# Transformer block on one core: prologue with w_mod's first part on one queue, one rstd for four tiles, two tiles' statistics on ScalarE, K before Q, and no early stop for PV without V

## The chip, the cores and the metric

The kernel runs on one core of a Trainium2 chip. The metric is the device time in microseconds (us), as the median of several runs. The engines are named as in the profile: PE (TensorE, matmuls; PEld is its weight load), ACT (ScalarE), DVE (VectorE), POOL (GpSimd), SP (SyncE, which here only issues transfers).

## The reference

One transformer block with adaptive layer norm, on 2048 tokens of 512 values, 32 heads of 16 and a feed-forward width of 1792, all in bfloat16:

```
mod = silu(c) @ w_mod                      # six rows of 512: sa, ca, ga, sb, cb, gb
h   = layernorm(x) * (1 + ca) + sa
q, k, v = split(h @ wqkv)                  # 32 heads of 16
x   = x + ga * (softmax(q k^T / 4) v @ wo)
h   = layernorm(x) * (1 + cb) + sb
x   = x + gb * ((gelu(h @ w_gate) * (h @ w_up)) @ w_down)
```

## The kernel before, in words

A recorder takes every instruction in the order of the program, keeps for every tile who wrote and read it, and adds the semaphore waits that follow. Two engines that read the same PSUM bank are ordered as well: the later reader waits for the earlier. Each engine executes its instructions in the order in which they were recorded.

The program has three stretches.

The *prologue* (`prologue`, L558 on) loads c, x and the first columns of the weights, computes silu(c), the first eight modulation columns (`mod_cols`, 32 matmuls that read w_mod's first 1024 columns), the layer norm statistics of the first four token tiles, their normalized copies, their transposes and modulation (into `hT`), and K and Q of the first 128 columns for the first 512 tokens. Statistics of a tile are two DVE instructions (`ln_stat`); `ln_rstd` is two small POOL instructions for a range of tiles; `ln_norm` is one DVE instruction per tile. `warm_up(n)` gives PE n dummy products, of four matmuls each. Transfers are issued on two queues, SP's and ACT's; a transfer issued on ACT occupies ACT's instruction stream while it is issued. The first scores need K (`km[0]`, the tile kme, in which every second head is masked) and Q (`qT`).

The *stream* (`stream`, L1185 on) is written by a planner at build time. The scores are worked through in items: one item is one head's scores for 128 keys and 512 queries, one PSUM bank. A round is four items, the four heads of one unit for one key tile. PE writes scores into three banks, then into two (later three) others; ACT turns each set into E with one exp. At positions from 30 on, some rounds (quads) are taken off ACT: DVE computes their four banks into uint16 and makes the shifted copies, partly with POOL. PV products (E times V, into `ps_pv` or a score bank) follow when their four items are there. In the first 128 items the planner goes through four groups of four key tiles for the first two units, so K of a new group of tokens must be there every 32 items.

Between scores the planner puts side work on PE: V, transposes, K and Q of later tokens and columns, then the modulation rows, and later the output projection and the feed-forward part of finished query sets. Side work is paced by a credit that grows with each item taken (the side work still to do, divided by the items up to its due position). It is forced when something needs it (`require`). Small steps on DVE, POOL, ACT and SP hang in a list of tasks and are taken when the planner's model has the engine free. `side_first` (L752) is the first piece of side work: V of the first tokens, then the statistics and norms of the other twelve tiles as tasks, then for each group its transposes, K and V.

`pv_next` lists the PV rounds that could run. If V of the round is not computed, it has this rule, where `tq` is the time at which the next score banks are free and `pos` the number of items taken:

```python
if ("v", r * (512 // u[3]) // 4, u[1] // 2) not in self.have:
    if tq is not None and pos < SOON:
        break
    x = 0.0
```

A candidate with `x = 0.0` counts as ready; if it is taken, `pv` forces the side work up to V. It is taken when PE's last instruction used the array in column strips (as V's products do) and the credit is at most 1536, or when no score banks can be free soon.

The *tail* (`tail`) finishes the last two query tiles.

Of the kernel before, what the change touches and what calls it, by code (L numbers as in the profile page):

```python
# [5 lines left out]
ACT = mybir.ActivationFunctionType  # L6
ALU = mybir.AluOpType
# [6 lines left out]
P = 128  # L14
S_TOK = 2048
D = 512
# [53 lines left out]
URGENT = 6  # L70
LAG = 40
SOLO = 2
SOON = 12
CLOSE = 48
BACK = 8
END = (0, None)
# [397 lines left out]
class _Kernel(_Recorder):  # L474
# [12 lines left out]
    def alloc(self):  # L487
# [49 lines left out]
        self.st6 = sb("st6", [P, 2, 6], FP32)  # L537
        self.rstd = sb("rstd", [P, NT], FP32)
        self.half = sb("half", [P, 4], FP32)
        self.crow = dreg[:, 9 * D:10 * D]  # L540
        self.tcol = sb("tcol", [P, NDC], FP32)
        self.sc_bf = sb("sc_bf", [P, NDC], BF16)
        self.scbc = sb("scbc", [P, NDC, P], BF16)[:, :, :]
        self.modA = sb("modA", [P, 8], FP32)
# [13 lines left out]
    def prologue(self):  # L558
        sp, act, pe, dve, pool = "sp", "act", "pe", "dve", "pool"
        xv = self.A_x.rearrange("b (t p) d -> p (b t) d", p=P)  # L560
        wmv = self.w_mod.rearrange("(a p) n -> p a n", p=P)
        wqv = self.A_wqkv.rearrange("(a p) (k n) -> p a k n", p=P, k=3)
        wq4 = self.wqkv.rearrange("p a (k n) -> p a k n", k=3)
        self.dma(sp, self.crow[0:1, :], self.c, "c")
        self.dma(act, self.xs[:, 0:2, :], xv[:, 0:2, :], "x0")
        self.dma(sp, self.xs[:, 2:4, :], xv[:, 2:4, :], "x1")
        self.dma(act, self.wmod[0][:, 0:2, :], wmv[:, 0:2, 0:1024], "wm0")
        self.dma(sp, self.wmod[0][:, 2:4, :], wmv[:, 2:4, 0:1024], "wm2")
        for k, q in ((1, sp), (0, act), (2, sp)):
            self.dma(q, wq4[:, :, k, 0:P], wqv[:, :, k, 0:P], "wq%d" % k)  # L570
        self.dma(act, self.xs[:, 4:8, :], xv[:, 4:8, :], "x2")
        self.dma(sp, self.xs[:, 8:12, :], xv[:, 8:12, :], "x3")
        self.dma(sp, self.xs[:, 12:16, :], xv[:, 12:16, :], "x4")
        for k in range(3):
            self.dma(sp, wq4[:, :, k, P:D], wqv[:, :, k, P:D], "wr%d" % k)
        self.dma(sp, self.wmod[1], wmv[:, :, 1024:3072], "wm1")

        self.memset(dve, self.warm, 0.0)
        self.memset(dve, self.ones, 1.0)
        self.memset(dve, self.half[:, :], -0.5)  # L580
        self.memset(dve, self.pv[:, :], 0.0)
        self.memset(dve, self.scp[:, SC - 1, :], 0.0)
        self.warm_up(7)
        self.memset(pool, self.ident[:, :], 0.0)
        self.affine_select(self.ident[:, :], [[-1, P]], ALU.not_equal, 1.0, 0, 1)
        self.memset(pool, self.rm4, 1.0)
        self.affine_select(self.rm4, [[-32, 4]], ALU.is_ge, 0.0, -16, 1)
        self.affine_select(self.rm4, [[32, 4]], ALU.is_ge, 0.0, 31, -1)
        self.reduce(self.rm[:, 1:2], self.rm4, mybir.AxisListType.X, ALU.add)
        self.ts(dve, self.rm[:, 0:1], self.rm[:, 1:2], -1.0, 1.0, ALU.mult, ALU.add)  # L590
        self.memset(pool, self.vaug[:, :, :].rearrange("p t (h c) -> p t h c", c=VW)[:, :, :, DH:VW], 1.0)

        for dc in range(NDC):
            self.mm(self.scp[:, 0, dc:dc + 1], self.crow[0:1, P * dc:P * dc + P], self.ones[0:1, 0:1])
        self.warm_up(14)
        self.act(self.tcol[:, :], self.scp[:, 0, 0:NDC], ACT.Tanh, scale=0.5)
        for t in range(2):
            self.ln_stat(t)
        self.ln_rstd(0, 2)
        self.stt(self.tcol[:, :], self.tcol[:, :], 1.0, self.scp[:, 0, 0:NDC], ALU.add, ALU.mult)  # L600
        self.ts(dve, self.sc_bf[:, :], self.tcol[:, :], 0.5, None, ALU.mult)
        for t in range(2, 4):
            self.ln_stat(t)
        self.ln_rstd(2, 4)
        self.mod_cols(self.scp[:, 1, 0:8], 0)
        for t in range(4):
            self.ln_norm(t, self.tb1[:, 0, t, :])
        self.copy(dve, self.modA[:, :], self.scp[:, 1, 0:8])
        self.ts(dve, self.modA[:, 4:8], self.modA[:, 4:8], 1.0, None, ALU.add)
        self.warm_up(3)  # L610
        kb, qb = self.pv[:, :], self.scp[:, 1, :]
        for dc in range(NDC):
            pt = self.scp[:, 2 + dc, :].bitcast(BF16)[:, 0:512]
            for t in range(4):
                self.transpose(pt[:, P * t:P * t + P], self.tb1[:, 0, t, P * dc:P * dc + P], self.ident[:, :])
            self.modulate(dve if dc % 2 == 0 else act, self.hT[:, dc, 0:512], pt, self.modA, dc)
        for dci in range(NDC):
            self.proj_part(kb, 512, 0, dci)
            self.proj_part(qb, 0, 0, dci)
        self.ts(dve, self.km[0][:, 0, 0:512], kb, self.rm[:, 0:1], None, ALU.mult)  # L620
        self.act(self.qT[:, 0, 0:512], qb, ACT.Copy, scale=Q_SCALE)
        self.ts(dve, self.km[1][:, 0, 0:512], kb, self.rm[:, 1:2], None, ALU.mult)

    def warm_up(self, n):
        for _ in range(n):
# [38 lines left out]
                        self.sc_bf[:, dc:dc + 1], start=(dc == 0), stop=(dc == NDC - 1))  # L664
        self.whole = False

    def proj_part(self, bank, col, g, dci):
        self.mm(bank, self.wqkv[:, dci, col:col + P], self.hT[:, dci, 512 * g:512 * g + 512],
                start=(dci == 0), stop=(dci == NDC - 1))

    def done(self, key):
        if not self.dry:
# [79 lines left out]
    def side_first(self):  # L752
        def stats(tiles):
            for t in tiles:
                self.task([lambda t=t: self.ln_stat(t)], ("st", t))

        def norms(t0):
            g = t0 // 4
            self.task([("pool", lambda: self.ln_rstd(t0, t0 + 4))]
                      + [lambda t=t: self.ln_norm(t0 + t, self.tb1[:, g % 2, t, :]) for t in range(4)], ("ln", g),  # L760
                      self.after([("st", t) for t in range(t0, t0 + 4)]))
        yield from self.side_v(0, 0)
        if not self.dry:
            stats([4, 5, 6, 7])
            norms(4)
        if not self.dry:
            stats([8, 9, 10, 11])
            norms(8)
            stats([12, 13, 14, 15])
        for g in range(1, 4):  # L770
            yield from self.until(("ln", g))
            for h in range(2):
                yield from self.side_t(lambda t: self.tb1[:, g % 2, t, :], 4, h,
                                       lambda dc: self.hT[:, dc, 512 * g:512 * g + 512], self.modA)
            if g == 1 and not self.dry:
                norms(12)
            yield from self.side_k(g, 0)
            yield from self.side_v(g, 0)
# [406 lines left out]
    def stream(self):  # L1185
# [76 lines left out]
        def pv_next():  # L1262

            res = []
            for k in open_rounds():
# [5 lines left out]
                    break  # L1271
                src = [self.slot[g0 + j] for j in range(4)]
                if ("v", r * (512 // u[3]) // 4, u[1] // 2) not in self.have:
                    if tq is not None and pos < SOON:
                        break
                    x = 0.0
                else:
                    x = self.probe(lambda: pv(rnd, 0, src))
# [457 lines left out]
```

## Time and profile before

| | |
|---|---|
| median of 3 runs | 807.23 us (806.83 to 807.97) |
| the profiled execution | 806.83 us, span 805.0 us |
| PE, DVE, ACT, POOL busy | 749.6, 671.0, 773.7, 277.7 us |
| first exp starts | 13.51 us |
| exps of two banks | 407, 1122 ns each |
| exps of three banks | 271, 1542 ns each |
| granted PE clock, mean | 0.999 |

A line of a group of instructions reads: source line, engine, operation, output tile and input tile with their shapes, count, then busy time in us and mean ns of one, then the idle time of the engine just before them and what ended most of it. A timeline line reads: start in us, length in us, engine, line, operation, tiles, count, and in brackets the idle time before it and its releaser; neighbouring instructions of one kind are merged. The line of GB/s divides the time asked for into 40 equal slices. A line of transfers ends with the size of one and the time from issue to landing. Line numbers are mostly those of helpers (L368 a matmul, L381 an ACT instruction, L393 a DVE or POOL tensor-scalar, L421 and L425 the statistics, L635 and L637 `ln_rstd`), so tiles tell the instructions apart: `ps_sc` holds scores and prologue products, `ps_mi` side work and warm-ups, `mreg` w_mod at first, `wreg` wqkv, `hreg` hT, `xs` x, `dreg` the normalized copies.

### The profile page before, as it was taken

The page shows a single profiled execution, that of the slowest core. Times are in us where ns is not written, and L with a number is a line of the kernel's source. Part 1 is how long each engine was busy: PE and PEld are TensorE (multiplying, and loading weights), DVE is VectorE, ACT ScalarE, POOL GpSimd, SP SyncE. Part 2 cuts the span into 40 slices and gives each one's busy share as a digit, 9 for nine tenths or more (in the row PEclk, how much of TensorE's full clock was granted, in tenths as well). Part 3 has the DMA queues.
Part 4 walks back from the last instruction along what each step waited for, and adds up shares of the span by engine and source line. Part 5 has one row for each costly group of instructions (what it writes and reads, how often), then busy time and mean ns, then how long its engine had stood idle before and what let it go on. Part 6 is the DMA issues. An engine that isn't in the chain of part 4 may idle for free.

```text
span 805.0 us, 27412 instructions
## 1 busy us (share of the span) xinstructions
PE 749.6 (93%) x12250; PEld 267.6 (33%) x12254; DVE 671.0 (83%) x1216; ACT 773.7 (96%) x728; POOL 277.7 (34%) x172
## 2 busy tenths in 40 slices
PE   8899999998899999999999899999999899999987
PEld 3333333322222222222222222222344342454455
DVE  7878898978898989988688998989778986677873
ACT  5999999999999999999999999999999999999982
POOL 3110335365546172456556346134262010000310
PEclk9999999999999999999999999999999999999999
DMA  9101000000022121111003111110123221120100
GB/s 310 58 9 19 10 10 16 10 16 10 16 55 68 35 55 36 48 41 29 24 27 108 36 52 51 48 42 17 42 59 89 63 75 37 34 75 14 23 9 14
DMA packets 58632, 36.03 MB, mean 45 GB/s; under 512 B 17977, under 2 KB 55090, under 8 KB 58514
## 3 DMA queue, kind: packets, MB, share of 16 engines
q1 hardware_dynamic: 56914, 32.84, 15.0%
q8 instruction: 96, 1.57, 0.8%
q10 hardware_dynamic: 1600, 1.44, 0.6%
q14 instruction: 22, 0.18, 0.1%
HBM read 29.62 MB, written 2.61 MB: 40 GB/s over the span
## 4 chain that ended last, share of the span: by engine, by line
ACT 89%; PE 8%; DVE 3%; issue 0%; DVEq 0%
ACT E L381 85%; PE ps_sc L368 4%; ACT wreg L381 3%; PE ps_mi L368 3%; PE ps_pv L368 1%; DVE mreg L393 1%; DVE kmo L402 0%; DVE xs L385 0%; DVE wreg L385 0%; PE ps_sc L372 0%; DVE hreg L393 0%; ACT L381 0%; DVE vaug L402 0%; DVE dreg L393 0%; DVE kme L393 0%
## 5 line engine op out<-in xcount | busy, mean ns | idle before, releaser
L381 ACT ACTIVATE E<-ps_sc 128x1024 bf16<-128x1024 f32 (+2 forms) x686 | 748.2, 1282 | 15.6 <-PE ps_sc L368 15.0
L393 POOL TENSOR_SCALAR mreg<-dreg 128x2048 uint16<-128x2048 uint16 x93 | 175.3, 1902 | 260.7 <-DVE mreg L393 105.7
L393 DVE TENSOR_SCALAR dreg<-ps_sc 128x512 uint16<-128x512 f32 x253 | 171.6, 685 | 34.3 <-PE ps_sc L368 31.8
L368 PE MATMUL ps_sc<-qT,kme 32*128 32x512 bf16 (+2 forms) x1313 | 168.3, 332 | 18.3 <-ACT E L381 15.1
L368 PE MATMUL ps_sc<-qT,kmo 32*128 32x512 bf16 (+2 forms) x1313 | 173.7, 332 | 9.7 <-ACT E L381 8.5
L368 PE MATMUL ps_pv<-E,vaug 128*17 128x512 bf16 (+2 forms) x2112 | 150.4, 327 | 0.8 <-DVE osb L402 0.5
L393 POOL TENSOR_SCALAR mreg<-mreg 128x2048 uint16<-128x2048 uint16 x46 | 86.7, 1902 | 138.8 <-DVE mreg L393 47.1
L368 PE MATMUL ps_pv<-mreg,vaug 128*17 128x512 bf16 (+2 forms) x1704 | 121.6, 337 | 1.7 <-DVE mreg L393 1.0
L393 DVE TENSOR_SCALAR mreg<-ps_sc 128x512 uint16<-128x512 f32 x126 | 85.4, 686 | 18.9 <-PE ps_sc L368 17.5
L368 PE MATMUL ps_mi<-wreg,mreg 128*32 128x512 bf16 (+1 forms) x1280 | 92.4, 372 | 4.4 <-DVE wreg L398 1.3
L368 PEld LDWEIGHTS ps_sc<-qT,kme 32*128 32x128 bf16 x1313 | 45.0, 91 | 143.7 <-ACT E L381 115.4
L368 PEld LDWEIGHTS ps_sc<-qT,kmo 32*128 32x128 bf16 x1313 | 45.7, 91 | 127.8 <-ACT E L381 109.3
L393 DVE TENSOR_SCALAR mreg<-dreg 128x2048 uint16<-128x2048 uint16 x117 | 76.8, 682 | 1.7 <-PE ps_pv L368 1.4
L368 PEld LDWEIGHTS ps_pv<-E,vaug 128*17 128x17 bf16 x2112 | 43.9, 89 | 61.5 <-issue 48.8
L368 PEld LDWEIGHTS ps_pv<-mreg,vaug 128*17 128x17 bf16 x1704 | 38.1, 89 | 36.8 <-issue 13.2
L402 DVE CAST wreg<-ps_mi 128x512 bf16<-128x512 f32 x49 | 33.5, 684 | 10.5 <-PE ps_mi L368 10.3
L368 PEld LDWEIGHTS ps_mi<-wreg,mreg 128*32 128x32 bf16 x1280 | 26.7, 95 | 44.0 <-issue 18.8
L368 PE MATMUL ps_mi<-hreg,wreg 128*32 128x512 bf16 x480 | 39.5, 385 | 0.0
L393 DVE TENSOR_SCALAR mreg<-mreg 128x2048 uint16<-128x2048 uint16 x59 | 38.4, 682 | 1.1 <-PE ps_pv L368 1.0
L398 DVE SCALAR_TENSOR_TENSOR wreg<-wreg,ps_mi 128x512 bf16<-128x512 bf16 x49 | 33.4, 682 | 6.5 <-PE ps_mi L368 5.1
L635 POOL TENSOR_SCALAR mv<-mv 128x4 f32<-128x4 f32 (+2 forms) x11 | 2.6, 239 | 94.5 <-DVE mv L425 93.9
L385 DVE TENSOR_TENSOR wreg<-wreg 128x1024 bf16<-128x1024 bf16 (+1 forms) x56 | 34.1, 616 | 0.5
(149 smaller groups left out, 670.8 us busy)
## 6 DMA issues: line engine op xcount, KB each, us to landing
mreg<-in_B_w_up_dram SPq DMA_DIRECT2D x22, 256.0 KB, 2.9
mreg<-in_B_w_gate_dram SPq DMA_DIRECT2D x15, 256.0 KB, 3.0
rb<-scr_rec SPq DMA_DIRECT2D x96, 32.0 KB, 1.8
dreg<-in_B_w_down_dram SPq DMA_DIRECT2D x9, 256.0 KB, 3.0
mreg<-in_w_mod_dram SPq DMA_DIRECT2D x1, 2048.0 KB, 13.3
mreg<-in_B_w_down_dram SPq DMA_DIRECT2D x8, 256.0 KB, 2.7
out_dram<-xs SPq DMA_DIRECT2D x16, 128.0 KB, 1.7
osb<-osb SPq DMA_DIRECT2D x48, 32.0 KB, 2.0
```

The costliest lines, as they stand in the source:

```text
L368: return self.rec("pe", lambda e: e.matmul(out, lhsT, rhs, start=start, stop=stop, tile_position=tp), [lhsT, rhs], [out], cost=(n, int(rhs ...
L381: return self.rec("act", lambda e: e.activation(out, in_, func, scale=scale, **kw), rd, wr, cost=self.cost("act", out, [in_], "act"))
L385: return self.rec(eng, lambda e: e.tensor_tensor(out, a, b, op), [a, b], [out], cost=self.cost(eng, out, [a, b], "tt"))
L393: return self.rec(eng, lambda e: e.tensor_scalar(out, a, s1, s2, **kw), rd, [out], cost=self.cost(eng, out, [a], "ts"))
L398: return self.rec("dve", lambda e: e.scalar_tensor_tensor(out, a, s, b, op0=op0, op1=op1), rd, [out], cost=self.cost("dve", out, [a, b], " ...
L402: return self.rec(eng, lambda e: e.tensor_copy(out, in_), [in_], [out], cost=self.cost(eng, out, [in_], "ts"))
L635: self.rec("pool", lambda e: e.tensor_scalar(v, v, EPS, None, op0=ALU.add), [v], [v], cost=200)
```

## The change

- w_mod's first 1024 columns were loaded as two halves, one on each queue; now as one transfer on SP. The second x transfer of ACT's queue follows x0 directly; of the three first wqkv parts the K part goes to SP and the Q and V parts to ACT; the last x transfer moves from SP to ACT.
- The statistics of tiles 4 and 5 are computed in the prologue on ACT, as two passes each with a sum (`act_stat`), and turned into mean and variance by three small DVE instructions (`act_stat_fin`). Those of tiles 6 and 7 are computed in the prologue on DVE, after the modulation.
- One `ln_rstd` for tiles 0 to 3 in place of two for two tiles.
- Warm-ups: 16 in place of 14 before the modulation columns, 2 behind them and none in place of 3 before the transposes.
- K and Q of the first 512 tokens: K's products all first, into a score bank; then ACT makes kmo and DVE kme from it; then Q's products. Before, the products alternated, DVE made kme and kmo, and K's bank was ps_pv.
- `side_first`: the norms of tiles 4 to 7 are put in the list before V, and need no statistics any more.
- The rule with SOON is gone from `pv_next`.

```diff
-        self.dma(act, self.wmod[0][:, 0:2, :], wmv[:, 0:2, 0:1024], "wm0")
-        self.dma(sp, self.wmod[0][:, 2:4, :], wmv[:, 2:4, 0:1024], "wm2")
-        for k, q in ((1, sp), (0, act), (2, sp)):
-            self.dma(q, wq4[:, :, k, 0:P], wqv[:, :, k, 0:P], "wq%d" % k)
+        self.dma(sp, self.wmod[0], wmv[:, :, 0:1024], "wm0")
         self.dma(act, self.xs[:, 4:8, :], xv[:, 4:8, :], "x2")
+        for k in range(3):
+            self.dma(sp if k == 1 else act, wq4[:, :, k, 0:P], wqv[:, :, k, 0:P], "wq%d" % k)
         self.dma(sp, self.xs[:, 8:12, :], xv[:, 8:12, :], "x3")
-        self.dma(sp, self.xs[:, 12:16, :], xv[:, 12:16, :], "x4")
+        self.dma(act, self.xs[:, 12:16, :], xv[:, 12:16, :], "x4")
...
-        self.warm_up(14)
+        self.warm_up(16)
         self.act(self.tcol[:, :], self.scp[:, 0, 0:NDC], ACT.Tanh, scale=0.5)
+        for t in range(4, 6):
+            self.act_stat(t)
         for t in range(2):
             self.ln_stat(t)
-        self.ln_rstd(0, 2)
         self.stt(self.tcol[:, :], self.tcol[:, :], 1.0, self.scp[:, 0, 0:NDC], ALU.add, ALU.mult)
         self.ts(dve, self.sc_bf[:, :], self.tcol[:, :], 0.5, None, ALU.mult)
         for t in range(2, 4):
             self.ln_stat(t)
-        self.ln_rstd(2, 4)
+        self.ln_rstd(0, 4)
         self.mod_cols(self.scp[:, 1, 0:8], 0)
+        self.warm_up(2)
...
-        self.warm_up(3)
-        kb, qb = self.pv[:, :], self.scp[:, 1, :]
...
-        for dci in range(NDC):
-            self.proj_part(kb, 512, 0, dci)
-            self.proj_part(qb, 0, 0, dci)
-        self.ts(dve, self.km[0][:, 0, 0:512], kb, self.rm[:, 0:1], None, ALU.mult)
-        self.act(self.qT[:, 0, 0:512], qb, ACT.Copy, scale=Q_SCALE)
-        self.ts(dve, self.km[1][:, 0, 0:512], kb, self.rm[:, 1:2], None, ALU.mult)
+        for t in range(6, 8):
+            self.ln_stat(t)
+        self.proj_k(0, 0, self.scp[:, 2, :], "both")
+        self.proj_q(0, 0, self.scp[:, 3, :], act)
+        self.act_stat_fin(4, 6)
+
+    def act_stat(self, t):
+        self.act(self.E[:, 0, :], self.xs[:, t, :], ACT.Copy, accum=self.asum[:, 0, t - 4:t - 3])
+        self.act(self.E[:, 0, :], self.xs[:, t, :], ACT.Square, accum=self.asum[:, 1, t - 4:t - 3])
+
+    def act_stat_fin(self, a, b):
+        m, q, t = self.asum[:, 0, a - 4:b - 4], self.asum[:, 1, a - 4:b - 4], self.nwt[:, a:b]
+        self.ts("dve", self.mv[:, a:b, 0], m, 1.0 / D, None, ALU.mult)
+        self.stt(t, m, 1.0 / D, self.mv[:, a:b, 0], ALU.mult, ALU.mult)
+        self.stt(self.mv[:, a:b, 1], q, 1.0 / D, t, ALU.mult, ALU.subtract)
...
+    def proj_k(self, g, dc, bank, how):
+        self.proj(bank, 512 + P * dc, g)
+        sl = slice(512 * g, 512 * g + 512)
+        if how == "both":
+            self.act(self.km[1][:, dc, sl], bank, ACT.Copy, scale=self.rm[:, 1:2])
...
+        self.ts("dve", self.km[0][:, dc, sl], bank, self.rm[:, 0:1], None, ALU.mult)
...
-                      self.after([("st", t) for t in range(t0, t0 + 4)]))
+                      self.after([("st", t) for t in range(max(8, t0), t0 + 4)]))
+        if not self.dry:
+            norms(4)
         yield from self.side_v(0, 0)
-        if not self.dry:
-            stats([4, 5, 6, 7])
-            norms(4)
...
-                    if tq is not None and pos < SOON:
-                        break
```

## The prediction

> **What bounds the kernel now.** I read the busy shares first, then the chain that ended last, then the groups of instructions by shape.
>
> ```profile
> PE 749.6 (93%) x12250; PEld 267.6 (33%) x12254; DVE 671.0 (83%) x1216; ACT 773.7 (96%) x728; POOL 277.7 (34%) x172
> ...
> ACT 89%; PE 8%; DVE 3%; issue 0%; DVEq 0%
> ```
>
> ```profile
> L381 ACT ACTIVATE E<-ps_sc 128x1024 bf16<-128x1024 f32 x407 | 399.9, 1122 | 0.5 <-PE ps_sc L368 0.5
> L381 ACT ACTIVATE E<-ps_sc 128x1536 bf16<-128x1536 f32 x271 | 391.6, 1542 | 2.6 <-PE ps_sc L368 2.1
> L381 ACT ACTIVATE wreg<-wreg 128x1024 bf16<-128x1024 bf16 x21 | 24.0, 1158 | 0.0
> ```
>
> ACT carries the chain: once the first exp has started, the 686 exps follow each other with hardly an idle microsecond. So the time is the start of the first exp, plus the sum of the exps, plus the few gaps between them, plus a tail after 780 us that the diff does not touch. Next I read the timeline of ACT alone, from 12 us on, for the start and the gaps.
>
> ```profile
> 12.33 0.60 ACT L381 ACTIVATE qT<-ps_sc 128x512 bf16<-128x512 f32 x1 [0.91 <-PE ps_sc L368]
> 13.51 13.66 ACT L381 ACTIVATE E<-ps_sc 128x1536 bf16<-128x1536 f32 x12 [0.58 <-PE ps_sc L368]
> 28.70 31.57 ACT L381 ACTIVATE E<-ps_sc 128x1536 bf16<-128x1536 f32 x31 [1.53 <-PE ps_sc L368]
> ```
>
> The first exp starts at 13.51. There is one gap of 1.53 us, at 27.17, where the first four key tiles are used up; the timeline of all engines shows K of the second four arriving late:
>
> ```profile
> 27.14 0.69 DVE L402 CAST kmo<-ps_mi 128x512 bf16<-128x512 f32 x1 [0.38 <-PE ps_mi L368]
> 27.87 0.35 DVE L393 TENSOR_SCALAR kme<-kmo,rm 128x512 bf16<-128x512 bf16 x1
> 28.26 0.35 DVE L393 TENSOR_SCALAR kmo<-kmo,rm 128x512 bf16<-128x512 bf16 x1
> 28.28 0.39 PE L368 MATMUL ps_sc<-qT,kme 32*128 32x512 bf16 x1 [0.87 <-DVE kme L393]
> ```
>
> The change moves both numbers, and a third place between them. The prologue in the timeline (DVE, POOL, PE) and the transfers of the first 30 us give the prices:
>
> ```profile
> 7.66 0.95 PE L368 MATMUL ps_sc<-sc_bf,mreg 128*128 128x1 bf16 x32
> 8.54 0.83 PE L368 MATMUL ps_mi<-dreg 128*32 128x512 bf16 x12
> ```
>
> ```profile
> 18.70 0.24 POOL L635 TENSOR_SCALAR mv<-mv 128x4 f32<-128x4 f32 x1 [10.10 <-DVE mv L425]
> 19.02 1.03 POOL L637 TENSOR_TENSOR rstd<-mv,half 128x4 f32<-128x4 f32 x1
> ```
>
> ```profile
> GB/s 0 0 34 243 343 406 412 380 355 292 281 306 308 301 359 347 350 338 328 328 326 370 370 414 399 399 404 421 365 367 217 46 37 0 22 0 0 0 0 0
> ...
> mreg<-in_w_mod_dram ACTq DMA_DIRECT2D x1, 512.0 KB, 4.6
> mreg<-in_w_mod_dram SPq DMA_DIRECT2D x1, 512.0 KB, 5.8
> ```
>
> **The change, part by part.** *w_mod's first part on one queue.* Now its halves, issued at 1.24 and 1.67, land at 5.84 and 7.47, and the modulation columns start on PE at 7.66, 0.19 later. After, the whole 1.05 MB stands on SP behind c and x1, while ACT's queue carries x0, x2 and two wq parts. Adding up the 0.75 us slices above, the core had moved 1.85 MB by 7.5 us, 2.06 by 8.25, 2.29 by 9.0, 2.52 by 9.75, 2.75 by 10.5. It lands at the earliest when x0, x1, x2 and itself are in (2.10 MB: 8.4 us), at the latest when both queues have moved the 1.31 MB that SP's needs (2.62 MB: 10.1 us). I take the middle, 9.3: neither end is nearer to a row.
>
> [...]
>
> *One rstd for four tiles instead of two for two.* The last of the four aggregates ends at 7.40 in both. Four columns took 0.24 + 1.03 on POOL, with the norms starting 1.50 after the aggregate; four norms took 1.35 there (20.11 to 21.46). So 7.40 + 1.50 + 1.35 = 10.25 for the last norm, against 9.38 now.
>
> *The meeting of both on PE.* Columns from 9.5 to 10.4; two warm-ups behind them 0.5 (three took 0.76) to 10.9; the first quarter of the transposes 0.27, and 0.1 to the first modulate: 11.3, now 9.76. The norms (10.25) are then hidden; if the transfer lands by 8.7 they set 10.6 instead.
>
> *ACT's statistics for tiles 4 and 5.* Four passes of 0.60 to 0.70 (512 columns from PSUM, 598 ns; from SBUF, 695 ns), 2.8 at most, in an ACT gap of 5.16 before its first modulate. x2 should land between 5.84 and 7.5, where the w_mod halves landed, so they end by 10.3, before ACT's modulate at 11.5: nothing, unless x2 lands after 8.7; then microsecond for microsecond. ACT also issues five transfers instead of four. Four took 0.43 to 0.53 each; a fifth 0.5 to 1.36 (the rows of SP's later ones), so the table load and tanh come 0.1 to 0.9 later and DVE, which reaches tanh's reader at 5.42, waits 0.4 at most: hidden, as the norms have 0.6 to spare. SP loses two issues and x4; its later weight loads move up, nobody waits for them.
>
> [...]
>
> *K first, then Q; one more pass.* Now K and Q alternate and the last Q group starts at 11.89. After, from 11.3: ACT's two modulates (1.45, begun 0.21 behind DVE's) end at 12.96; K's last group starts at 13.06, and four Q groups of 0.215 follow, the last at 13.92, ending at 14.31. qT takes 0.60 on ACT: 14.36 to 14.96, now 12.33 to 12.93. Beside it ACT does K's odd copy first (13.5 to 14.1); the even copy on DVE must wait for that, since the recorder orders readers of a bank on different engines. It runs 14.2 to 14.95; behind it the two statistics of tiles 6 and 7 (2 x 0.87, from 12.3 to 14.05) are hidden, by 0.1 only. wq1 follows w_mod on SP; one such part took 1.6, which gives 11.1 to 11.8, beside the 11.9 at which K starts. First QK 0.14 after qT, exp 0.44 later: 15.55, **+2.05**, bounds +1.4 (w_mod hidden) and +2.85 (10.1).
>
> *SOON removed.* After two rounds of QK (5 items) the first PV round has its four slots, but V does not exist. Now the planner breaks off there. After, V's first part puts PE in column mode with credit 273 x 3 + 284 x 2 - 512 = 876, under 1536, so PV is placed at once, V is forced, and PV stands in PE's order ahead of the third QK. Its fourth matmul needs the second exp. QK then starts only when that exp has ended: 0.05 for the release (14.96 to 15.01), 0.32 between starts when the mode changes (19.53 to 19.85), 0.44 to the exp: **+0.8**. Ends: 0 (QK placed first) and 1.5 (PV also waits for V's cast, 0.69 more).
>
> *Statistics of 4 to 7 gone from the stream, norms put ahead of V.* POOL can start at 15.4 instead of 18.70, relative to the first exp 5 us earlier. The gap of 1.53 needs 1.5, so K is no longer late. What is late next at such a boundary? At the next one, 71.52, the gap is 0.38; I let that remain: **-1.15** (ends -1.53 and 0).
>
> *DVE freed.* 4 x 0.87 = 3.4 us of DVE work leave the stream. The planner may give DVE one quad more (four items off ACT, 4 x 1.34/3 = 1.8 us), or, replanned from other times, one less. I take 0, ends -1.8 and +1.8.
>
> Sum: 2.05 + 0.8 - 1.15 = +1.7. The profiled execution took 806.83 (805.0 of span, 1.8 around it), so 808.5; the median of the runs is 0.40 above it, so **808.9**.
>
> **The rivals.** *Freed DVE takes quads (ends on the other side).* Place: 28 to 37 us, where DVE's first bank of a quad (31.38) is six microseconds from the second (37.37), with statistics, norms and modulates between. For it: three of those statistics would be gone. Against: from 30 to 50 us DVE is busy 15.7 of 20, so free time alone does not make quads. Price 1.8 each: one gives 807.1, two 805.3, faster; it decides from the second.
>
> *The gap at 27 us stays*, because side work is paced by credit and forced only when needed: +1.15, 810.0; with the late transfer too, 810.9. Against: K's chain gains far more than the gap.
>
> *The prologue's delay is smaller*: w_mod hidden and the PV order harmless, so 1.4 + 0 - 1.15: about 807.5, no difference.
>
> *The two starts add up with a lost quad*: 808.9 + 1.8 = 810.7.
>
> **How the numbers follow.** Two runs of this kernel can be told apart from about 0.2%, 1.6 us. My sum has 0.45 (807.9 to 809.7: two thirds of it beyond 808.84); gap stays or quad lost 0.27, slower; smaller delay 0.10, same; quads taken 0.18, of which 0.12 faster. Faster 0.12, same 0.32, slower 0.56. The range leaves out a tenth on each side: the end with nearly two quads taken and the top of the lost-quad case, 806.4 to 811.2.
>
> **What would show it.** First exp near 15.5, modulation columns on PE near 9.5 (right if between 8.7 and 10.3); a gap of 0.8 before the third exp with PV ahead of QK in PE's order; no gap over 0.5 near 29 to 31; the count of DVE's uint16 reads of score banks within four of now. I am wrong if the exps change in number, or if w_mod lands before 8.4.

## The result and the profile after

The changed kernel takes 812.75 us (811.46 to 812.88, 4 runs) against 807.39 (806.83 to 807.97, 4 runs): a ratio of 1.0063, with a 95% interval of 1.0045 to 1.0080. It is 5.4 us slower. The forecast had the sign and the places, but 1.7 us; the time lies above the top of its range, 811.2.

The page of the changed kernel, busy times and the chain that ended last:

```profile
PE 749.8 (92%) x12266; PEld 268.0 (33%) x12270; DVE 673.1 (83%) x1224; ACT 779.3 (96%) x734; POOL 246.4 (30%) x153
...
ACT 90%; PE 7%; DVE 2%; DMA 1%; issue 0%; SPq 0%; DVEq 0%
```

ACT is the chain as before, and it is busy 5.6 us longer. The exps by shape (count, then busy us and mean ns):

```profile
L380 ACT ACTIVATE E<-ps_sc 128x1536 bf16<-128x1536 f32 x280 | 406.6, 1546 | 2.5 <-PE ps_sc L367 1.8 <-PE ps_mi L367 0.3
L380 ACT ACTIVATE E<-ps_sc 128x1024 bf16<-128x1024 f32 x396 | 393.3, 1126 | 0.9 <-PE ps_sc L367 0.8
```

280 x 3 + 396 x 2 = 1632 score banks go through ACT. Before, 271 x 3 + 407 x 2 and a single one made 1628. The four more are one quad that DVE no longer gets: its uint16 reads of score banks went from 420 (253 + 126 + 27 + 14, by tile) to 416 (244 + 124 + 32 + 16). The timeline of ACT:

```profile
7.89 0.63 ACT L380 ACTIVATE E<-xs 128x512 bf16<-128x512 bf16 x1 [2.79 <-DMA xs<-in_A_x_dram]
...
10.69 0.19 ACT L380 ACTIVATION_READ_ACCUMULATOR E<-xs 128x1 f32 x1
12.12 1.48 ACT L380 ACTIVATE hreg<-ps_sc,modA 128x512 bf16<-128x512 bf16 x2 [1.24 <-PE ps_sc L371]
14.66 0.69 ACT L380 ACTIVATE kmo<-ps_sc,rm 128x512 bf16<-128x512 f32 x1 [1.06 <-PE ps_sc L367]
16.05 0.60 ACT L380 ACTIVATE qT<-ps_sc 128x512 bf16<-128x512 f32 x1 [0.70 <-PE ps_sc L367]
17.23 2.37 ACT L380 ACTIVATE E<-ps_sc 128x1536 bf16<-128x1536 f32 x2 [0.58 <-PE ps_sc L367]
20.61 53.05 ACT L380 ACTIVATE E<-ps_sc 128x1536 bf16<-128x1536 f32 x51 [1.02 <-PE ps_sc L367]
```

The first exp starts at 17.23 in place of 13.51. There is a new gap of 1.02 before the third exp, and the 1.53 at 27 us is gone. PE's timeline shows why the start is late:

```profile
7.71 0.82 PE L367 MATMUL ps_mi<-dreg 128*32 128x512 bf16 x12
10.04 0.94 PE L367 MATMUL ps_sc<-sc_bf,mreg 128*128 128x1 bf16 x32 [1.51 <-DMA mreg<-in_w_mod_dram]
10.91 0.61 PE L367 MATMUL ps_mi<-dreg 128*32 128x512 bf16 x8
11.46 1.32 PE L371 MATMUL ps_sc<-ident,dreg 128*128 128x128 bf16 x16
12.70 3.29 PE L367 MATMUL ps_sc<-hreg,wreg 128*32 128x512 bf16 x32
```

PE sits idle for 1.51 us until w_mod has landed, and later the 16 transposes take 1.32 and the 32 products of K and Q 3.29. Before, the transposes took 1.07, and the same 32 products ran from 10.36 to 12.28:

```profile
9.31 1.07 PE L372 MATMUL ps_sc<-ident,dreg 128*128 128x128 bf16 x16
10.36 0.40 PE L368 MATMUL ps_pv<-hreg,wreg 128*32 128x512 bf16 x4
...
11.89 0.39 PE L368 MATMUL ps_sc<-hreg,wreg 128*32 128x512 bf16 x4
```

Stretches of one microsecond (length, busy time and count of PE, PEld, DVE, ACT and POOL, then the granted PE clock, the share of the DMA engines and GB/s) show the clock of that time:

```profile
11.00:12.00 1.00, 1.00 (x18) 0.57 (x18) 0.44 (x3) 0.00 (x0) 0.00 (x0) 1.00 1.10 347
12.00:13.00 1.00, 1.00 (x14) 0.67 (x15) 1.00 (x3) 0.89 (x2) 0.00 (x0) 0.56 1.10 344
13.00:14.00 1.00, 1.00 (x16) 0.36 (x16) 0.96 (x3) 0.59 (x1) 0.00 (x0) 0.50 1.10 331
14.00:15.00 1.00, 1.00 (x16) 0.43 (x12) 0.51 (x2) 0.34 (x1) 0.00 (x0) 0.50 1.12 334
15.00:16.00 1.00, 1.00 (x20) 0.36 (x12) 0.55 (x1) 0.34 (x1) 0.00 (x0) 0.73 1.08 333
```

The clock granted to PE is halved from 12.1 to 15.5 us. In the trace of before it is 1.00 in every such stretch from 4 to 40 us.

One table holds all profiled executions. The medians of before that the ratios refer to lie between 807.2 and 807.5. *First* is the start of the first exp. *Exps* is ACT's time from there to the table load at the end of the stream, less *gaps* (its idle stretches in the stream, as the timeline lists them). *Tail* is the rest of the span. Each row adds up to its span, as the tail is what is left.

| kernel | median us | ratio to before (95%) | first | exps | gaps | tail | span | banks on ACT |
|---|---|---|---|---|---|---|---|---|
| before | 807.39 | | 13.51 | 762.40 | 2.08 | 26.97 | 805.0 | 1628 |
| changed | 812.75 | 1.0063 (1.0045 to 1.0080) | 17.23 | 764.29 | 2.42 | 26.97 | 810.9 | 1632 |
| e1 warm-ups | 812.67 | 1.0059 (1.0040 to 1.0077) | 16.15 | 764.22 | 4.62 | 26.97 | 812.0 | 1632 |
| e2 queues alone | 809.76 | 1.0026 (1.0016 to 1.0036) | 15.19 | 762.43 | 2.08 | 26.96 | 806.7 | 1628 |
| e3 7 warm-ups | 810.31 | 1.0035 (1.0020 to 1.0050) | 13.43 | 762.74 | 4.25 | 26.96 | 807.4 | 1628 |
| e4 SOON back | 812.16 | 1.0047 (1.0031 to 1.0063) | 16.69 | 765.01 | 2.80 | 26.98 | 811.5 | 1632 |
| e5 changed again | 813.13 | 1.0071 (1.0057 to 1.0085) | 16.68 | 764.30 | 2.97 | 26.97 | 810.9 | 1632 |
| e6 101 quads | 813.86 | 1.0083 (1.0070 to 1.0097) | 13.50 | 769.07 | 2.08 | 26.97 | 811.6 | 1644 |
| e7 statistics back | 812.17 | 1.0058 (1.0045 to 1.0072) | 16.40 | 761.87 | 3.31 | 28.98 | 810.6 | 1624 |
| e8 no SOON | 808.67 | 1.0018 (1.0008 to 1.0027) | 14.72 | 760.82 | 1.64 | 28.98 | 806.2 | 1624 |
| e9 1 warm-up | 809.37 | 1.0032 (1.0018 to 1.0046) | 14.94 | 762.71 | 3.97 | 26.97 | 808.6 | 1628 |
| e10 changed, other plan | 808.31 | 1.0009 (1.0000 to 1.0018) | 15.72 | 756.85 | 4.66 | 29.75 | 807.0 | 1612 |
| e11 BACK = 9 | 802.99 | 0.9948 (0.9933 to 0.9963) | 13.58 | 755.64 | 2.72 | 28.97 | 800.9 | 1612 |
| e12 no SOON, other plan | 806.32 | 0.9988 (0.9975 to 1.0000) | 13.89 | 754.67 | 2.74 | 32.55 | 803.8 | 1608 |

Changed less before, by columns: 3.72 for the start, 1.89 for the exps, 0.34 for the gaps, 0 for the tail; 5.95 of span.

Only one execution of each kernel is profiled, but the mean granted clock of every execution is on record, and it tells how far the profiled one stands for the others. In the trace of the changed kernel the stretch at half clock lasts 3.413 us (12.121 to 15.534), which lowers the mean over some 806 us by 0.002; in the trace of before the last 1.95 us (from 803.007 on), 2.3 us behind PE's last product, are at half clock too and lower it by 0.0012. So I take it, as an estimate from these two traces, that a mean of 0.999 or 1.000 has no such stretch, 0.997 or 0.998 has one, and less has two or more. By it, seven of the nine executions of the changed kernel (four here, five in e5) have one and took 812.7 to 813.3 us; the other two have none and took 811.5 and 812.0. Of the 58 executions of before beside e1 to e12, 50 have none (median 807.2) and eight have one or two (median 808.85). Where the stretch lies is known for the profiled executions only.

### The profile page after: what moved, and what is told of

It is laid out like the page before. It is cut to its first block, busy times and chain, and to the rows that moved or that the text cites. A ratio compares the mean times of both kernels' runs of the same rounds, so it can differ in the third digit from the quotient of the medians.

```text
span 810.9 us, 27445 instructions
## 1 busy us (share of the span) xinstructions
PE 749.8 (92%) x12266; PEld 268.0 (33%) x12270; DVE 673.1 (83%) x1224; ACT 779.3 (96%) x734; POOL 246.4 (30%) x153
## 4 chain that ended last, share of the span: by engine, by line
ACT 90%; PE 7%; DVE 2%; DMA 1%; issue 0%; SPq 0%; DVEq 0%
ACT E L380 86%; PE ps_sc L367 4%; ACT wreg L380 3%; PE ps_mi L367 2%; DMA mreg<-in_w_mod_dram 1%; PE ps_pv L367 1%; DMA den<-scr_den 0%; PE ps_sc L371 0%; DVE hreg L392 0%; DVE kmo L401 0%; DVE wreg L384 0%; DVE dreg L392 0%; ACT L380 0%; SPq L431 0%; DVE kme L392 0%
## 5 line engine op out<-in xcount | busy, mean ns | idle before, releaser
L392 POOL TENSOR_SCALAR mreg<-dreg 128x2048 uint16<-128x2048 uint16 x88 | 165.9, 1901 | 268.2 <-DVE mreg L392 89.2
L392 DVE TENSOR_SCALAR dreg<-ps_sc 128x512 uint16<-128x512 f32 x244 | 164.9, 685 | 32.0 <-PE ps_sc L367 30.0
L367 PE MATMUL ps_sc<-qT,kmo 32*128 32x512 bf16 (+2 forms) x1314 | 171.5, 332 | 13.7 <-ACT E L380 12.5
L367 PE MATMUL ps_sc<-qT,kme 32*128 32x512 bf16 (+2 forms) x1301 | 170.9, 332 | 8.6 <-ACT E L380 7.2
L392 POOL TENSOR_SCALAR mreg<-mreg 128x2048 uint16<-128x2048 uint16 x34 | 64.3, 1901 | 188.6 <-DVE mreg L392 61.8
L392 DVE TENSOR_SCALAR mreg<-ps_sc 128x512 uint16<-128x512 f32 x124 | 84.7, 685 | 16.4 <-PE ps_sc L367 14.9
L392 DVE TENSOR_SCALAR mreg<-dreg 128x2048 uint16<-128x2048 uint16 x119 | 78.7, 687 | 1.7 <-PE ps_pv L367 1.5
L392 DVE TENSOR_SCALAR mreg<-mreg 128x2048 uint16<-128x2048 uint16 x71 | 47.2, 684 | 1.3 <-PE ps_pv L367 1.1
L367 PE MATMUL ps_sc<-xs,ident 128*32 128x512 bf16 x372 | 29.8, 385 | 16.3 <-ACT E L380 15.9
```

The costliest lines, as they stand in the source:

```text
L367: return self.rec("pe", lambda e: e.matmul(out, lhsT, rhs, start=start, stop=stop, tile_position=tp), [lhsT, rhs], [out], cost=(n, int(rhs ...
L392: return self.rec(eng, lambda e: e.tensor_scalar(out, a, s1, s2, **kw), rd, [out], cost=self.cost(eng, out, [a], "ts"))
```

## The experiments

These profiles leave two theories. *Clock*: the idle 1.5 us of PE halve its clock, and this costs about 1 us of the start on top of the late landing. *Banks*: the planner's new plan gives ACT four banks more, and that is the 1.89.

**e1: warm-ups up to the landing**

```diff
-        self.warm_up(16)
+        self.warm_up(23)
```

> The changed kernel with 23 warm-ups in place of 16 before the modulation columns, so that PE stays busy until w_mod has landed (9.9 us); w_mod lands when it did, and the plan of the stream is unchanged (276 or so quads and exps in the same order, 1632 banks on ACT). Theory 'clock': the granted PE clock was 0.50 from 12.2 to 15.5 us after PE had idled 1.51 us at 8.53; without the idle time it stays 1.00, the 16 transposes take 1.07 in place of 1.32 and the K and Q products 1.9 in place of 3.29, and the first exp starts near 16.2 in place of 17.23: the whole about 1.0 us shorter than the changed kernel, 811.7. Rival 'landing only' (the first exp is late because w_mod and the norms are late): first exp 17.2 or a little later, time unchanged at 812.7.

PE's timeline, and the line of ACT's that starts the stream:

```profile
6.68 2.98 PE L367 MATMUL ps_mi<-dreg 128*32 128x512 bf16 x52
9.66 0.94 PE L367 MATMUL ps_sc<-sc_bf,mreg 128*128 128x1 bf16 x32
10.53 0.61 PE L367 MATMUL ps_mi<-dreg 128*32 128x512 bf16 x8
11.08 1.07 PE L371 MATMUL ps_sc<-ident,dreg 128*128 128x128 bf16 x16
12.11 2.39 PE L367 MATMUL ps_sc<-hreg,wreg 128*32 128x512 bf16 x32
15.16 0.62 PE L367 MATMUL ps_mi<-xs,ident 128*32 128x512 bf16 x8 [0.66 <-DMA xs<-in_A_x_dram]
```

```profile
16.15 2.37 ACT L380 ACTIVATE E<-ps_sc 128x1536 bf16<-128x1536 f32 x2 [1.00 <-PE ps_sc L367]
```

No idle stretch, no halved clock in the prologue; transposes 1.07, products 2.39, and the first exp 1.08 earlier than in the first profile of the changed kernel. Some of that is the landing: from the start of the columns to the first exp it is 6.49 here against 7.19. What is late next shows too: the planner's fillers (dummy products that it puts between scores) read the last x tile, which the change put last on ACT's queue, and PE waits 0.66 for it in front of the first QK. The median did not move: this execution had two half-speed stretches in mid-stream, at 120 and 612 us (granted clock 0.99 from 100 to 700 us, mean 0.994), with 2.3 of gaps about them that the first profile had not (0.31, 0.92 and 0.19 new, the 0.34 grown to 1.19). The clock theory holds for the start. For the whole time the granted clocks split the four executions: two with no half-speed stretch took 811.8 and 812.3, as the two such executions of the changed kernel did (811.5 and 812.0), and two with one or more took 813.1 and 813.9. So the warm-ups are worth no more than the stretch that they avoid, and four executions are too few to say how often they avoid it.

**e2: the queues alone, in the kernel before**

```diff
-        self.dma(act, self.wmod[0][:, 0:2, :], wmv[:, 0:2, 0:1024], "wm0")
-        self.dma(sp, self.wmod[0][:, 2:4, :], wmv[:, 2:4, 0:1024], "wm2")
-        for k, q in ((1, sp), (0, act), (2, sp)):
-            self.dma(q, wq4[:, :, k, 0:P], wqv[:, :, k, 0:P], "wq%d" % k)
+        self.dma(sp, self.wmod[0], wmv[:, :, 0:1024], "wm0")
         self.dma(act, self.xs[:, 4:8, :], xv[:, 4:8, :], "x2")
+        for k in range(3):
+            self.dma(sp if k == 1 else act, wq4[:, :, k, 0:P], wqv[:, :, k, 0:P], "wq%d" % k)
         self.dma(sp, self.xs[:, 8:12, :], xv[:, 8:12, :], "x3")
-        self.dma(sp, self.xs[:, 12:16, :], xv[:, 12:16, :], "x4")
+        self.dma(act, self.xs[:, 12:16, :], xv[:, 12:16, :], "x4")
```

> The kernel before, with the transfers alone issued as in the changed kernel (w_mod whole on SP, x2 next on ACT's queue, x4 on ACT's). The plan of the stream is that of before (1628 banks on ACT). Both theories: w_mod lands near 9.9, the columns start near 10.0 in place of 7.66. Theory 'clock': PE idles 2.3 us from 7.74, the clock is halved some 2 us later for 3.3 us, and the first exp starts near 16.9 to 17.3 (2.4 for the landing, 1.0 to 1.4 for the clock): time near 811. Rival 'landing only': first exp 15.9, 809.8. A third view, that the queues are harmless and the merged rstd is what delays the start: first exp near 13.5, 807.4.

PE's and ACT's timelines:

```profile
9.36 0.94 PE L368 MATMUL ps_sc<-sc_bf,mreg 128*128 128x1 bf16 x32 [0.74 <-DVE dreg L393]
```

```profile
15.19 13.68 ACT L381 ACTIVATE E<-ps_sc 128x1536 bf16<-128x1536 f32 x12 [0.58 <-PE ps_sc L368]
30.40 42.44 ACT L381 ACTIVATE E<-ps_sc 128x1536 bf16<-128x1536 f32 x41 [1.53 <-PE ps_sc L368]
```

The columns start 1.70 later than before (9.36 for 7.66), the first exp 1.68 later, and everything behind it is the kernel before: in this execution the queues are a plain shift. I had expected 2.3 us of idle time; only 0.74 came, because w_mod landed at 9.3 and the 56 warm-up products took 4.07 in place of 3.21, and the clock stayed at 1.00. So this execution says nothing against the clock theory, but that 0.74 idle did no harm here. By the medians the queues cost 2.2 of the 5.4. The granted clocks split this: six executions without a half-speed stretch have a median of 809.0, 1.5 above before, which is the shift; the other four, with one, took 810.2 to 810.5.

**e3: seven warm-ups fewer, in the kernel before**

```diff
-        self.warm_up(14)
+        self.warm_up(7)
```

> The kernel before with 7 warm-ups in place of 14 before the modulation columns, so that PE idles about 1.4 us with all transfers where they were and the plan unchanged. Theory 'clock': the clock drops to 0.50 for about 3.3 us, some time after the idle stretch, and the first exp starts 0.8 to 1.7 later than 13.51; time 808.2 to 809.1. Rival 'landing only': idle PE costs nothing, first exp 13.5, 807.4.

Inconclusive for its purpose: PE's only marked wait was 0.20 us, the clock stayed up, and the first exp started at 13.43. The median is 2.8 higher all the same. In the profiled execution two half-speed stretches in mid-stream (269 and 771 us; mean clock 0.995) came with 2.2 of gaps. The granted clocks say that this is the rule with this kernel: one of its ten executions has one such stretch (0.998, 808.5 us, the fastest), the other nine have two or more (0.990 to 0.995). Why fewer warm-ups in the prologue should bring them stays open.

**e4: SOON back, in the changed kernel**

```diff
                 if ("v", r * (512 // u[3]) // 4, u[1] // 2) not in self.have:
+                    if tq is not None and pos < SOON:
+                        break
                     x = 0.0
```

> The changed kernel with the rule with SOON put back in the choice of PV rounds, prologue untouched. Theory of the prediction: PV no longer stands ahead of the third QK, so the gap of 1.02 before the third exp goes; the first exp stays at 17.2. The plan behind it is a different one (286 exps of three banks and 387 of two in place of 280 and 396, the same 1632 banks), so the seven saved exps may give another 0.7; expected 811.0 to 811.8. Rival 'the gap is made up later' (DVE or the next group of K becomes the bound): 812.7.

The gap before the third exp is gone, and none comes at the end of the first four key tiles either: the statistics in the prologue alone are enough for that. The clock was halved from 11.3 to 14.8 (PE idle 1.33 at 8.2), as in the changed kernel. The median is 812.16, 0.4 above the forecast; the profiled execution had two half-speed stretches in mid-stream again (452 and 503 us; granted clock 0.99 from 100 to 700 us), with 2.3 us of gaps about them. Like with like it is the gap that is saved: the two executions with one half-speed stretch took 811.0 and 811.7 (the changed kernel's seven 812.7 to 813.3), the one with none 810.5 (811.5 and 812.0). The seven exps fewer saved nothing: exps 765.01 against 764.29. Here it is the banks that count, not the instructions.

**e5: the changed kernel again**

Nothing was edited.

> The changed kernel as it is, once more, to see which of its numbers belong to one execution. If the stretch of halved PE clock in the prologue (12.2 to 15.6 us in the first profile) belongs to the kernel, it is here again and the first exp starts near 17.2. If it is a matter of where the idle 1.5 us fall in the clock's own rhythm (every stretch at half speed so far lasted 3.413 us, and one kernel with 2.3 us idle had none), it may be absent, and then the first exp starts near 16.1. Time 812.7 either way within 1.

Columns at 9.50 after 1.31 idle, clock halved from 11.4 to 14.9, first exp at 16.68. (The kernel "with 2.3 us idle" that the expectation names is e2, where 2.3 was the forecast and 0.74 the measured idle time.) From the columns to the first exp it is 7.18, in the first profile 7.19, in e4 7.18: the halved clock belongs to more than one execution. (e10, whose prologue is the same, shows that it need not come.) The 0.55 between the two first exps is w_mod's landing (9.37 for 9.87).

**e6: four quads fewer, in the kernel before**

```diff
-                    elif (cand and self.quad_free
+                    elif (cand and len(vec) < 404 and self.quad_free
```

> The kernel before with at most 101 quads given to DVE in place of 105; everything up to there is as before, and 16 score banks more go to ACT (1644 in place of 1628). Theory 'banks': ACT is the chain, so each bank costs what an exp costs per bank, 1.34/3 = 0.45 us, and the time grows by 7.1, to 814.6. Then the four banks that the changed kernel has more on ACT explain 1.8 of its 5.3. Rival 'DVE is the second chain': with four quads less DVE the stream runs with fewer waits, and the time grows by less than half of that, under 811.

The exps by shape:

```profile
L381 ACT ACTIVATE E<-ps_sc 128x1536 bf16<-128x1536 f32 x284 | 408.1, 1555 | 2.5 <-PE ps_sc L368 2.1
L381 ACT ACTIVATE E<-ps_sc 128x1024 bf16<-128x1024 f32 x396 | 389.0, 1125 | 0.5 <-PE ps_sc L368 0.5
```

284 x 3 + 396 x 2 = 1644 banks, the same gaps and tail, and exps 769.07 against 762.40: 6.67 for 16 banks, 0.42 each. The time grows by 6.5. ACT's banks go straight into the time; the DVE work that goes away gives nothing back. The prediction's 1.8 for a quad is 1.67 here. The changed kernel's four banks are then 1.7 of its 1.89.

**e7: the statistics back in the stream, in the changed kernel**

```diff
-        for t in range(4, 6):
-            self.act_stat(t)
...
-        for t in range(6, 8):
-            self.ln_stat(t)
...
-        self.act_stat_fin(4, 6)
...
-                      self.after([("st", t) for t in range(max(8, t0), t0 + 4)]))
-        if not self.dry:
-            norms(4)
+                      self.after([("st", t) for t in range(t0, t0 + 4)]))
         yield from self.side_v(0, 0)
+        if not self.dry:
+            stats([4, 5, 6, 7])
+            norms(4)
```

> The changed kernel with the statistics of tiles 4 to 7 back in the stream (none on ACT, none behind the modulation; the list of side work as before); queues, merged rstd, K before Q and the missing SOON rule stay. The planner then gives DVE 424 banks in place of 416, ACT 1624 in place of 1632. Theory 'banks': 8 x 0.45 = 3.6 less than the changed kernel; the gap at the end of the first four key tiles returns (+1.5); first exp 15.6 to 17.0; about 810.5. Rival 'the statistics on ACT or behind the modulation delay the first exp': first exp back below 15 and more than 1.5 of the time saved there. Rival 'the moved statistics help': time above 813.

Exps 2.42 less than in the changed kernel for eight banks (3.3 at 0.42). From the columns (10.34, idle 0.91 before them) to the first exp it is 6.06, with the transposes (1.07) and the products (2.38) as fast as in e1, where the clock was 1.00. I had forecast 6.05 for this stretch in the changed kernel. The gap at the end of the first four key tiles did not return, although the statistics are where they were. And the tail is 2.0 longer, which no theory had: 28.98. The median, 812.17, lies 1.7 above the forecast; the tail is the largest part of that. Three of the four executions have one or two half-speed stretches; the one without took 810.3. The eight banks say more: e7 is the changed kernel with these statistics put back (and the list of side work with them), and its plan gives ACT 1624 banks in place of 1632. Taking the statistics out of the stream, which frees DVE, cost DVE two quads.

**e8: no SOON, in the kernel before**

```diff
-                    if tq is not None and pos < SOON:
-                        break
```

> The kernel before without the SOON rule, nothing else. First exp 13.5 as before. PV ahead of the third QK: a gap of 0.8 to 1.0 before the third exp. The planner gives DVE 424 banks in place of 420, so ACT has 1.8 less to do. Theory 'banks': 807.5 + 0.9 - 1.8 = 806.6. Rival 'SOON is worth its gap and no more': 808.4.

ACT's timeline:

```profile
14.72 2.37 ACT L381 ACTIVATE E<-ps_sc 128x1536 bf16<-128x1536 f32 x2 [0.58 <-PE ps_sc L368]
18.11 28.34 ACT L381 ACTIVATE E<-ps_sc 128x1536 bf16<-128x1536 f32 x27 [1.02 <-PE ps_sc L368]
46.63 14.22 ACT L381 ACTIVATE E<-ps_sc 128x1024 bf16<-128x1024 f32 x14 [0.17 <-PE ps_sc L368]
```

Leaving out the rule is enough to make the gap of 1.02, and it also removes the gap of 1.53, with the statistics still in the stream. So either edit removes it; my reason (the statistics) was enough, but not needed. The four banks fewer on ACT are 1.6 less of exps, but they came with a tail of 28.98, and the two cancel: gaps and exps 2.0 less, tail 2.0 more. The first exp was 1.2 late in this execution, because w_mod landed late (columns at 8.76) with the prologue of before; the median is 1.3 above before. This execution is the fastest of its ten and the only one without a half-speed stretch, so that stretch is in the median too.

**e9: one warm-up, in the kernel before**

```diff
-        self.warm_up(14)
+        self.warm_up(1)
```

> The kernel before with 1 warm-up in place of 14 before the modulation columns; all transfers as before, the plan unchanged (1628 banks). PE then idles from about 4.8 to 7.6 us. (With 7 warm-ups the idle stretch was too short to tell: two pieces of a few tenths.) Theory 'clock': after more than 1.3 us of idle time the granted clock falls to 0.50 for 3.413 us within the next 3 us, and what PE does then takes twice as long: the first exp starts 0.5 to 1.7 later than 13.5, with the columns no later than before. Rival 'idle PE costs nothing': first exp 13.5 or earlier.

PE's timeline, two stretches of it by microseconds, and ACT's:

```profile
7.65 0.90 PE L368 MATMUL ps_sc<-sc_bf,mreg 128*128 128x1 bf16 x30 [1.58 <-DMA mreg<-in_w_mod_dram]
8.48 1.12 PE L368 MATMUL ps_mi<-dreg 128*32 128x512 bf16 x12
9.53 1.89 PE L372 MATMUL ps_sc<-ident,dreg 128*128 128x128 bf16 x16
```

```profile
9.00:10.00 1.00, 1.00 (x13) 0.47 (x6) 0.50 (x3) 0.00 (x0) 0.00 (x0) 0.50 1.17 309
10.00:11.00 1.00, 1.00 (x13) 1.00 (x11) 0.54 (x1) 0.40 (x1) 0.00 (x0) 0.50 1.09 330
```

```profile
14.94 2.37 ACT L381 ACTIVATE E<-ps_sc 128x1536 bf16<-128x1536 f32 x2 [0.58 <-PE ps_sc L368]
```

All transfers and the columns (7.65) are where they were; PE idled 0.72 and 1.58 before them, the clock was halved from 8.9 to 12.3, the transposes took 1.89, and the first exp came 1.43 later. This is the clock by itself, without the change. It is not in every execution: by their mean clocks three of the seven have a half-speed stretch (810.1 to 812.9 us) and four have none (808.7 to 809.4). Why those four are still 1.5 to 2.2 slower than before stays open.

**e10: another plan for the changed kernel**

```diff
+        cand = [k for i, k in enumerate(cand) if i not in (66,)]
```

> The changed kernel with one of the rounds that may go to DVE (the 67th) struck from the list. The planner then takes another way and gives DVE 436 banks in place of 416, ACT 1612 in place of 1632; the prologue is that of the changed kernel. Theory 'banks': at the 0.42 us a bank that sixteen banks cost, 8.3 less than the changed kernel: 804.6, under the kernel before although its first exp starts 3 us later. Rival 'DVE becomes the bound' (gaps in the exps take it back): above 809.

Twenty banks fewer on ACT: exps 7.44 less than in the changed kernel (8.3 forecast). But the tail is 2.8 longer and the gaps 2.2 more, so the time is 808.31, short of 804.6, and 0.1% above before with an interval that just touches it. The tail and the gaps gave 5.0 of the 7.4 back; that DVE became the bound, as the rival had it, is not what happened (above 809 forecast for it). The prologue is that of the changed kernel, yet here PE idled only 0.89 before the columns at 9.65, the clock stayed at 1.00, and the first exp came at 15.72: 6.07 from the columns, where three other executions of this prologue took 7.18.

**e11: one constant of the planner, in the kernel before**

```diff
-BACK = 8
+BACK = 9
```

> The kernel before with one constant of the planner changed: quads may be opened with a backlog of fewer than 9 DVE steps in place of 8. ACT gets 1612 banks in place of 1628; first exp 13.5 as before. Theory 'banks': 16 x 0.42 = 6.7 less than before: 800.7. Rival 'DVE becomes the bound': no faster than 806.

```profile
L381 ACT ACTIVATE E<-ps_sc 128x1024 bf16<-128x1024 f32 x428 | 421.9, 1125 | 0.9 <-PE ps_sc L368 0.9
L381 ACT ACTIVATE E<-ps_sc 128x1536 bf16<-128x1536 f32 x252 | 366.7, 1551 | 2.7 <-PE ps_sc L368 2.1 <-PE ps_mi L368 0.3
```

252 x 3 + 428 x 2 = 1612 banks in these groups by shape; exps 6.76 less than before, 0.42 a bank once more, the tail 2.0 longer, the time 802.99, 0.9948 of before (0.9933 to 0.9963). The forecast, 800.7, left out the tail, and is missed by 2.3. This beats both kernels.

**e12: no SOON and another plan, in the kernel before**

```diff
+        cand = [k for i, k in enumerate(cand) if i not in (72,)]
...
-                    if tq is not None and pos < SOON:
-                        break
```

> The kernel before without the SOON rule and with the 73rd candidate round struck from the list: 1608 banks on ACT in place of 1628, DVE 440. First exp 13.5; a gap of 1.0 before the third exp in place of 1.5 at the end of the first four key tiles. Theory 'banks': 20 x 0.42 = 8.3 less than before, 799; if the tail is 2.0 longer, as it was with the other kernel without the rule, 801. Rival 'DVE becomes the bound': no faster than 806.

The fewest banks, exps 7.73 less than before, and a tail of 32.55 that takes 5.6 of it back: 806.32, in place of the 799 to 801 forecast. In ACT's timeline the tail opens with a wait of 4.86; behind it eight of PE's products took 2.36 from 779.37 on, where later eights took 1.04 (with the mean clock of 0.997, one stretch at half clock):

```profile
772.60 0.20 ACT L381 ACTIVATE tcol<-tcol 128x1 f32<-128x1 f32 x1
777.67 0.60 ACT L381 ACTIVATE xs<-ps_sc 128x512 bf16<-128x512 f32 x1 [4.86 <-DVE E L393]
```

With this plan ACT's first gelu (781.76) comes behind the last xs tile it writes (777.67); before, a first gelu came at 782.31 and the xs tile at 784.71. All ten executions have at least one half-speed stretch (0.992 to 0.997).

## Why the prediction was wrong, step by step

*What bounds the kernel, and the sum of start, exps, gaps and tail*: right for the start, the exps and the gaps: sixteen banks more on ACT made the time 6.5 longer (e6), and ACT's gaps in the stream stay between 1.6 and 4.7 in all fourteen executions. The tail, which the sum left out, stayed at 26.97 in the changed kernel, but other plans made it up to 32.55.

*w_mod on one queue*: right. 9.3 was forecast for the landing, the middle of two ends and so in part luck; it came at 9.87 in the first profile and at 9.37 in the second. e2 shows it as a shift of 1.7. No profile with these queues shows a landing near the early end, 8.4: columns between 9.36 and 10.34.

*One rstd*: right and hidden. The norms ended at 10.06 (10.25 forecast), the columns at 10.98.

*Statistics on ACT*: right and hidden. Four passes took 0.63 each with a read of the accumulator of 0.19 behind each; they ended at 10.88, and ACT then waited 1.24 for PE.

*K first, then Q*: the working was right at full clock (6.05 from the columns to the first exp; 6.06 in e7, 6.07 in e10, 6.49 in e1 with its 0.66 wait for the last x tile), and w_mod's late landing was 0.54 of the miss (columns at 10.04 for 9.5). **Here the prediction failed first: this step prices PE's products and transposes at the durations of before, and lets PE wait for w_mod at no cost beyond the wait.** Where PE idled 1.3 to 1.5 us (both profiles of the changed kernel and e4), its clock was halved for 3.4 us and the stretch took 7.18: 1.1 more. e9 makes the same happen without the change, and e1 avoids it with more warm-ups. The upper end of the start (+2.85) held no such case, and the start was +3.72.

What the traces show of the idle time and the clock: 1.3 to 1.6 us of idle time were followed by half speed in all four profiled prologues that had them (1.51 and 1.31 in the changed kernel, 1.33 in e4, and 1.58 in e9, which idled 0.72 more just before), and 0.74, 0.89 and 0.91 in none of three (e2, e10, e7).

*SOON*: right. +0.8 forecast, 1.02 measured, and e8 and e4 show it alone. The wait, though, was not the one that the sum was made of (the second exp): what I had put at the far end, PV waiting for V's cast, is what happened, and PE waited 0.80 for it.

*The gap at 27 us*: gone as forecast, but e8 shows that the late PV takes it away as well. The allowance of 0.38 for the next boundary was too small: new gaps of 0.18, 0.66, 0.22 and 0.34 came, so -0.68 in place of -1.15.

*DVE freed, taken at 0*: **the second failure.** The new plan has one quad less, and the exps took 1.89 longer, just outside the end of +1.8. The rival that DVE takes quads had the sign wrong, and the case "a quad lost" had a part of 0.27 only. Edits of a single number move the plan by 16 and 20 banks (e11, e10; 0.4 us each), so this term's own spread was larger than the whole forecast; zero was its middle, not its likely size. e7 puts the loss down to the statistics that left the stream (1624 banks with them in it, 1632 without); why the planner then gives DVE less was not traced. The prediction's own sign of being wrong came as well: the exps changed in number, from 679 to 676.

Sum: 2.05, 0.8, -1.15 and 0 were 3.72, 1.02, -0.68 and 1.89. The halved clock alone does not carry the miss: the two executions of the changed kernel without it took 811.5 and 812.0, still above 811.2. Less the quad's 1.9 the median would have been 810.9, inside the range (an estimate from the table).

Slips in the working that moved nothing: the "686 exps" count seven gelus of the tail with them; the credit is 875, not 876; 4 x 0.87 is 3.5; x2 landed near 7.9 in the first profile, after the 7.5 allowed, and ACT's statistics ended at 10.88 in place of 10.3, still ahead of its modulate.

## What to carry to other kernels

When a change makes TensorE wait for a transfer, price what TensorE does after the wait at half speed too (here from 1.3 us of idle time on), or give it something to do until the data is there. When a planner writes the schedule, count first what its new plan puts on the bounding engine: here a bank is 0.42 us, and one constant was worth 4 us, more than most of the edits. And look at the end of the stream as well; a plan that saves 8 us of exps gave 5.6 back in the tail.

## What the runs showed of the hardware

In the trace of the changed kernel the granted clock is 1.00 for 6.827 us (from 5.294 on), 0.50 for 3.413 (12.121 to 15.534) and 1.00 for 795.305; in that of before it is 1.00 for 798.719 (4.288 to 803.007). To 0.1 us these times are 2, 1, 233 and 234 times 3.413. The half-clock stretches in the prologues of e4, e5 and e9, added up from stretches of one microsecond, are 3.42 long each. By the mean clocks (0.994, 0.995, 0.993, 0.997 and 0.998) such stretches also come in mid-stream in some executions (e1, e3 and e4 two each, e7 and e10 one), with gaps of 0.8 to 1.4 us about each; none was seen between prologue and tail in the two profiles of the changed kernel, nor in before, e2, e6, e8, e9, e11 and e12. What sets them off stays open. In the 3.413 us just ahead of the half-clock stretch PE was busy for only 2.08 us in the changed kernel (8.71 to 12.12) and for 1.42 in e9 (5.47 to 8.88). But stretches of that length with 2.16 us busy (before, 267.11 to 270.52) and 2.04 (the changed kernel, 346.63 to 350.04) were followed by a clock of 1.00.

The same first transfers land at different times from one execution to the next: with the prologue of before, the columns (in e3, e9 and e12 all but the first two products) ran from between 7.6 and 8.8 on, with the changed queues from between 9.36 and 10.34 on, and the first exp shifts with them.
